# Reading the moving columns of float32r matmuls as two halves in turn, in a channel-attention and GELU-FFN kernel

## The chip, the core and the metric

The kernel runs on one NeuronCore of a Trainium2 chip. The metric is the device time of one execution, in microseconds (us). The engines are TensorE (PE in the profile; its weight loads are shown apart as PEld), VectorE (DVE), ScalarE (ACT), GpSimd (POOL, hardly used here) and SyncE (SP), whose queue issues the transfers between device memory and SBUF.

## The reference

For each of four batches an attention over channels, then a feed-forward net over all tokens:

```python
# q, k, v: (4, 6080, 256) float32; w_in: (256, 2048); w_out: (2048, 256)
qn = q / (norm(q, axis=1) + 1e-6)
kn = k / (norm(k, axis=1) + 1e-6)
s = kn.transpose(0, 2, 1) @ qn / tau          # (4, 256, 256): channels by channels
a = exp(s - s.max(-1)); a /= a.sum(-1) + 1e-9
x = (v @ a).reshape(24320, 256)
h = x @ w_in
out = (0.5 * h * (1 + erf(h / sqrt(2)))) @ w_out
```

## The kernel before

**The algebra.** The attention matrix `a` of a batch is multiplied into `w_in` first (`w_product`, L704 to L712), so that the two layers of the net are two products: v times the batch's own weights, then GELU, then `w_out`. Each value is held as a sum of two float32r numbers, a high and a low part, and a product of two such values is three matmuls: low weights by high columns, high by high, high by low. Those threes are the lines L885 to L887 (first layer), L1017 to L1019 (second layer), L1001 to L1003 (second layer, plain form), L829 to L831 and L963 to L965 (the first two chunks of the first batch), and L710 to L712. The scores of the batches after the first are summed by L460 and L462; those of the first batch use plain float32 matmuls (L417, L429).

**The tiling.** The 6080 tokens of a batch are cut into 12 chunks (`CHUNKS`), whose halves are 256 columns wide, and 240 in chunks 10 and 11. A chunk goes through four groups g = 0 to 3 of 512 hidden units. Chunks 0 and 1 of the first batch are done apart, in a simpler loop; the remaining 46 chunks make 184 groups (`steps`). In each group the first layer is computed by seven products instead of eight (a Strassen-Winograd scheme, `do`): 7 x 2 x 3 = 42 matmuls. The second layer has two forms:

- the *crossed* one (`CROSS`, L1017 to L1019), again seven products, 42 matmuls of 256 columns. It needs sums of the activations, which VectorE and ScalarE make (`t_add` L925 to L929, `t_hi` L932, `t_lo` L936), and four banks of PSUM that are joined at the chunk's end (`join_ops`);
- the *plain* one (L1001 to L1003), eight products as 24 matmuls of 512 columns, without those sums, needing one low part more (`lo`, L918).

`plain_out` says which form a group takes: all four groups of chunk (0, 2), and the last group of the chunks for which `MIXED` (L302) is true, which are those with b < 3 and odd c, and (3, 11).

**The order.** The second layer of a group is interleaved on TensorE with the first layer of the next (`row` and `outs` in the last loop). The products of the attention matrix, the score sums of the next batch and the preparation of the next chunk's v are put among the groups by `put(n, kind, ...)` and `spread(n, kind, time)`: a kind ("act0", "dve1", "o5", ...) names a place within the group. The plan gives the program order on which dependencies rest. TensorE keeps that order; for ScalarE, VectorE and the transfers, `Order.schedule` then simulates the plan with the costs of `Order.cost` (L108 to L134), lets each engine take the ready instruction that is due first, and writes the order found into the program. For a float32r matmul of k columns `cost` gives:

```python
return .4427 * k + 3.4 + 1.5 * (k <= H), .4427 * k + 170
```

**Names for the steps of the change.** `wins` holds a group's part of `w_in`, `whs`/`wls` the batch's weights, `vhi`/`vlo` a chunk's v with its sums, `his`/`los` the activations, `gs` the whole activations from which the low parts are taken, `hls` the split q and k. `sacc` is the score sum in SBUF, 256 columns for the high terms and 256 for the cross terms, which are added at L619. The moving operand of a matmul is its third argument; all of them run through their columns from the first to the last.

Of the kernel before, what the change touches and what calls it, by code (L numbers as in the profile page):

```python
# [13 lines left out]
ALU = mybir.AluOpType  # L14
# [3 lines left out]
B, N, C = 4, 6080, 256  # L18
DFF = 2048
# [59 lines left out]
class Order:  # L79
# [32 lines left out]
    def cost(self, ins, reads, writes):  # L112
        n = max([x[3] for x in reads + writes] + [1])
        psum = any(x[0][0] in ("pa", "pb", "px", "pz", "po0", "po1", "po2", "po3") for x in reads)
        if ins.engine == PE:
            k = reads[0][3] if reads else 1
            if ins.ins[0].dtype == F32:
                return (max(1.69 * k, 112.0),) * 2
            return .4427 * k + 3.4 + 1.5 * (k <= H), .4427 * k + 170
        if ins.engine == DVE:  # L120
            t = n / .96 + 66
            if type(ins).__name__ == "InstTensorCopy" and not psum:
                t = n / 1.92 + 66
            return t, t + 90
        if ins.engine == ACT:
            t = .855 * n + (48 if psum else 80)
            return t + 90 * (len(ins.outs) > 1), t + 105
        return 60, n * 512 / BANDWIDTH
# [171 lines left out]


def MIXED(b, c):  # L302
    return b < 3 and c % 2 or (b, c) == (3, 11)


NARROWS = (4, 9)
# [9 lines left out]
A21, B12 = -1, T1  # L316
PLAIN = (((1, 0), ((A11, B11), (A12, B21))), ((0, 0), ((A21, B11), (A22, B21))),
         ((1, 1), ((A11, B12), (A12, B22))), ((0, 1), ((A21, B12), (A22, B22))))


@with_exitstack
def channel_attention_gelu_ffn(ctx, tc, qk, kqt, vt, tau, w_in, w_out, out):
# [100 lines left out]
    def qk_fill():  # L423
        state["fill"] = s = ps_o.tile([P, NCT, C], F32, name="po0")
        for i in range(FILL * JS):
            js, j = divmod(i, JS)
            raw = raws[1, js]
            for m in range(NCT):
                marks["fill"] = nc.tensor.matmul(  # L429
                    s[:, m], raw[:, j, 0, m * P:(m + 1) * P], raw[:, j, 1], start=(i == 0 and m == 0),  # L430
                    stop=(i == FILL * JS - 1), skip_group_check=True)
                yield
        acc = state["sacc"] = pm.tile([P, NCT, NT], F32, name="sacc")
        nc.gpsimd.memset(acc[:, :, C:], 0.0)
        nc.vector.tensor_copy(out=acc[:, :, 0:C], in_=s)


    def sum_up(nps, acc, start, stop):
# [16 lines left out]
    def burst(b, k, m):  # L455
        cs = slice(m * P, (m + 1) * P)
        s = state["burst"] = spare()
        ops = [(hls[b, k * NB + t], j) for t in range(NB) for j in range(JS)]
        for i, (hl, j) in enumerate(ops):
            nc.tensor.matmul(s, hl[:, 0, j, 0, cs], hl[:, :, j, 1], start=(i == 0), stop=False,  # L460
                             skip_group_check=True)
            nc.tensor.matmul(s[:, 0:C], hl[:, 1, j, 0, cs], hl[:, 0, j, 1], start=False,  # L462
                             stop=(i == len(ops) - 1), skip_group_check=True)

    def burst_sum(k, m):
# [141 lines left out]
    def softmax(first, pool, name):  # L607
# [5 lines left out]
        for m in range(NCT):  # L613
            t = pm.tile([P, C], F32, name=f"t{m}")
            if first:
                nc.scalar.copy(out=t, in_=state["s"][m])
            else:
                s = state["sacc"]
                nc.vector.tensor_tensor(out=t, in0=s[:, m, 0:C], in1=s[:, m, C:2 * C], op=ALU.add)  # L619
            ts.append(t)  # L620
        nsum = state.pop("nsum")
        if first:
# [82 lines left out]
    def w_product(b, g, m, pwt):  # L705
        eh, el = state["e"]
        win = wins[b, g]
        cs = slice(m * P, (m + 1) * P)
        for d in range(NCT):
            nc.tensor.matmul(pwt, eh[:, d, cs], win[:, 0, d], start=(d == 0), stop=False)  # L710
            nc.tensor.matmul(pwt, eh[:, d, cs], win[:, 1, d], start=False, stop=False)
            nc.tensor.matmul(pwt, el[:, d, cs], win[:, 0, d], start=False, stop=(d == NCT - 1))  # L712

    def w_scale(tmp, m, pwt):
        nc.scalar.activation(out=tmp[:, 2 * m:2 * m + 2], in_=pwt.rearrange("p (q r c) -> p r q c", q=2, r=2),
# [109 lines left out]
    def product(u, a, v, ps, start, stop):  # L825
        g, q = divmod(u, 2)
        hi, lo = vops[v]
        wh, wl = (t[:, q] for t in w_slot(g, a))
        nc.tensor.matmul(ps, wl, hi, start=start, stop=False, skip_group_check=True)  # L829
        nc.tensor.matmul(ps, wh, hi, start=False, stop=False, skip_group_check=True)  # L830
        marks["product"] = nc.tensor.matmul(ps, wh, lo, start=False, stop=stop, skip_group_check=True)  # L831

    def gelu(src):
        at = state["at"] = (state.get("at", -1) + 1) % 5
# [26 lines left out]
    def chunk_ops(b, c, g, n):  # L861
# [11 lines left out]
        def do(i):  # L873
            a, v = ORDER[i]
            at = VSLOT[v]
            if i == 0:
                new("one", ps_h, "pb" if n % 2 else "pa")
            if i == 1:
                state["spare"] = "pa" if n % 2 else "pb"
                new("two", ps_h, state["spare"])  # L880
            ps = t[("one", "two", "one", "x", "one", "z", "one")[i]]
            for q in range(2):
                o = ps[:, q]
                start, stop = i < 2 and q == 0, i not in (0, 2, 4)
                nc.tensor.matmul(o, wls[g][:, a, q], vh[:, at, :h], start=start, stop=False, skip_group_check=True)  # L885
                nc.tensor.matmul(o, whs[g][:, a, q], vh[:, at, :h], start=False, stop=False, skip_group_check=True)  # L886
                nc.tensor.matmul(o, whs[g][:, a, q], vl[:, at, :h], start=False, stop=stop, skip_group_check=True)  # L887

        def x_copy():
            new("x", ps_x, "px")  # L890
# [59 lines left out]
    def pair_out(u, blocks):  # L950

        wo = wos[0, 0, u]
        t0, n = PAIRS[0]
        for j in range(2):
            for i in (1, 0):
                gh, gl = blocks[i, j]
                for c in range(NCT):
                    if u == 0 and i == 1:
                        po[j, c] = ps_o.tile([P, NT], F32, name=f"po{2 * j + c}")
                    o = po[j, c]  # L960
                    cs = slice(c * P, (c + 1) * P)
                    first, last = u == 0 and i == 1, u == NU - 1 and i == 0
                    nc.tensor.matmul(o, wo[:, 1, i, cs], gh, start=first, stop=False)  # L963
                    nc.tensor.matmul(o, wo[:, 0, i, cs], gh, start=False, stop=False)
                    nc.tensor.matmul(o, wo[:, 0, i, cs], gl, start=False, stop=last)  # L965
                    if last:
                        if c == 0:
                            osb = pg.tile([P, NCT, NT], F32, name="osb", bufs=1)
                            nc.scalar.copy(out=osb[:, 0], in_=o)
                        else:  # L970
                            nc.vector.tensor_copy(out=osb[:, 1], in_=o)
                            send(0, t0 + j * n, n, osb, osb)
                    yield

    def chunk_out(b, c, g, n):
# [13 lines left out]
        if plain_out(b, c, g):  # L989
            for i in (1, 0):  # L990
                for k in range(NCT):
                    form = {(0, 0): "A11", (0, 1): "A12", (1, 0): "A21", (1, 1): "A22"}[k, i]
                    for q in range(2):
                        def op(i=i, k=k, q=q, form=form):
                            w = wos[key + (form,)]
                            at = SLOT["B22"] if i else p_slot(n)
                            mh, ml = (m.rearrange("p i (q n) -> p i q n", q=2)[:, at:at + 2, q, :h] for m in (his, los))
                            start = first and i == 1 and q == 0
                            stop = last and i == 0 and q == 1
                            o = acc(k)  # L1000
# [7 lines left out]
        for i, (name, form, v) in enumerate(CROSS):  # L1008
            def op(i=i, name=name, form=form, v=v):
                k, half = PLACE[name]  # L1010
                o = acc(k)[:, half]
                w = wos[key + (form,)]
                starts = s_first and name in ("P3", "P4", "P1", "P5")
                stops = s_last and (k > 1 or last)
                for q in range(2):
                    mh, ml = (halves(m[:, SLOT[v]], h)[:, q] for m in (his, los))
                    nc.tensor.matmul(o, w[:, 1, q], mh, start=starts and q == 0, stop=False, skip_group_check=True)  # L1017
                    nc.tensor.matmul(o, w[:, 0, q], mh, start=False, stop=False, skip_group_check=True)  # L1018
                    nc.tensor.matmul(o, w[:, 0, q], ml, start=False, stop=stops and q == 1, skip_group_check=True)  # L1019
                if i % 2 or i == 6:  # L1020
                    load_part()
# [200 lines left out]
    for b in range(1, B):  # L1222
# [23 lines left out]
        for g in range(NWG):  # L1246
# [13 lines left out]
            for m in range(NCT):  # L1260
                put(n, "PE", product, m)
                put(n, "PEact", scale, m)
            put(n, "dve3", lambda tmp=tmp: w_adds(tmp["t"]))
            for i in range(2):
                put(n + 1, "act", lambda i=i, g=g, tmp=tmp: w_hi(g, tmp["t"], i))
                put(n + 1, "dve2", lambda i=i, g=g, tmp=tmp: w_lo(g, tmp["t"], i))
# [34 lines left out]
    for n, (b, c, g) in enumerate(steps):  # L1301
# [27 lines left out]
            put(n + 2, "dve1", ship, *((1,) if last else ()))  # L1329
        else:  # L1330
            put(n + 1, "o2", copy, 0)
            put(n + 1, "act2", copy, 2)
            put(n + 2, "act", copy, 3)
            put(n + 2, "dve1", join, "u1")
            put(n + 2, "dve1", join, "u23")
# [14 lines left out]
    for n, (b, c, g) in enumerate(steps):  # L1350
# [6 lines left out]
        for item in row:  # L1357
# [15 lines left out]
                e[item] = now + D  # L1373
            now += D
        assert not extra
        spread(n, "load", start + 0.02)
        spread(n, "act0", start + 0.03)
        spread(n, "dve0", start + 0.9)
# [10 lines left out]
        spread(n, "dve2", e[4] + .75)  # L1389
        spread(n, "o5", ends[5] + .05)  # L1390
        spread(n, "o2", ends[2] + .05)
        at(e[4] + .8, gelu_hi, "B11")
        at(e[4] + 1.3, gelu_whole, "B11")
        at(e[4] + 1.85, lo, "B11")
# [69 lines left out]
```

## Time and profile before

| | |
|---|---|
| median of 3 runs | 2144.01 us (2140.47 to 2144.54) |
| the profiled execution | 2140.3 us, its span 2138.5 us |
| granted TensorE clock, mean | 0.999 |
| matmul passes | 16444 |
| read from and written to device memory | 456.39 MB and 37.49 MB, 231 GB/s over the span |

The profile is of one execution. Its page gives each engine's busy time, and groups of instructions by line: tile written <- tiles read, number, busy time, mean duration of one, and the idle time of the engine just before them with what ended it. Matmuls overlap: one starts while the one before still drains, so the distance between two starts, not the printed duration, is what a pass takes of the engine. A float32 matmul shows as two passes; a float32r matmul as one. The timeline lists instructions by their start, the table of windows gives busy times in stretches of the span, and the list of waits says which instruction waited for which.

### The profile page before, as it was taken

How to read it: one execution, taken by the hardware profiler on the slowest of the kernel's cores; microseconds unless marked ns; L12 is line 12 of the kernel's file. 1: busy time of each engine (PE TensorE's matmuls, PEld its weight loads, DVE VectorE, ACT ScalarE, POOL GpSimd, SP SyncE). 2: the span in 40 equal slices, each digit the busy share in tenths (PEclk: the TensorE clock that was granted, in tenths of full speed). 3: DMA queues.
4: the chain of work that ended last, by engine and by line, in shares of the span. 5: the costliest groups of instructions: out<-in, count | busy, mean ns of one | idle time of the engine just before them, and what ended most of it. 6: DMA issues, size and time to landing. Idle time of an engine off the chain costs nothing.

```text
span 2138.5 us, 41862 instructions
## 1 busy us (share of the span) xinstructions
PE 2110.8 (99%) x16444; PEld 2035.4 (95%) x16444; DVE 1947.6 (91%) x2840; ACT 1656.4 (77%) x2768; POOL 1.3 (0%) x8
## 2 busy tenths in 40 slices
PE   8999999999999999999999999999999999999999
PEld 7788999999999999999999999999999999999999
DVE  6987999998899999999989999989999999999997
ACT  6656787788888888788887777777778777777776
POOL 0000000000000000000000000000000000000000
PEclk9999999999999999999999999999999999999999
DMA  9547777786887877877766666665566566656665
GB/s 380 184 125 265 266 252 247 273 273 211 273 283 244 279 245 248 276 235 269 255 216 227 217 230 209 224 215 198 197 208 218 186 197 211 230 193 223 220 202 185
DMA packets 159476, 496.61 MB, mean 232 GB/s; under 512 B 16304, under 2 KB 26544, under 8 KB 157232
## 3 DMA queue, kind: packets, MB, share of 16 engines
q1 hardware_dynamic: 159280, 493.94, 68.5%
q8 instruction: 129, 2.11, 0.4%
q14 instruction: 67, 0.55, 0.1%
HBM read 456.39 MB, written 37.49 MB: 231 GB/s over the span
## 4 chain that ended last, share of the span: by engine, by line
PE 88%; DVE 4%; DMA 4%; ACT 3%; issue 1%; SPq 0%; DVEq 0%; ACTq 0%
PE po L1017 12%; PE po L1019 12%; PE po L1018 12%; PE pa L885 5%; PE pb L885 5%; PE pa L887 5%; PE pa L886 5%; PE pb L887 5%; PE pb L886 5%; PE pz L887 2%; PE pz L885 2%; PE pz L886 2%; PE px L887 2%; PE px L885 2%; PE px L886 2%; PE pa L460 1%
## 5 line engine op out<-in xcount | busy, mean ns | idle before, releaser
L1017 PE MATMUL po<-his,wo 128*128 128x256 f32 (+1 forms) x2268 | 632.4, 279 | 1.5 <-DMA wo<-keep_out 1.4
L1019 PE MATMUL po<-los,wo 128*128 128x256 f32 (+1 forms) x2268 | 631.3, 278 | 0.3 <-DVE los L936 0.3
L1018 PE MATMUL po<-his,wo 128*128 128x256 f32 (+1 forms) x2268 | 631.3, 278 | 0.0
L932 ACT CAST his<-gs 128x1024 fp32r<-128x1024 f32 (+1 forms) x324 | 338.0, 1043 | 137.9 <-DVE gs L929 130.1
L918 DVE TENSOR_TENSOR los<-gs,his 128x512 fp32r<-128x512 f32 (+1 forms) x574 | 387.4, 683 | 54.8 <-ACT gs L912 40.2
L1017 PEld LDWEIGHTS po<-his,wo 128*128 128x128 f32 x2268 | 426.0, 188 | 5.6 <-DMA wo<-keep_out 2.1
L1018 PEld LDWEIGHTS po<-his,wo 128*128 128x128 f32 x2268 | 426.1, 188 | 0.8
L1019 PEld LDWEIGHTS po<-los,wo 128*128 128x128 f32 x2268 | 426.1, 188 | 0.6 <-DVE los L936 0.5
L936 DVE TENSOR_TENSOR los<-gs,his 128x1024 fp32r<-128x1024 f32 (+1 forms) x324 | 392.6, 1212 | 25.3 <-ACT his L932 23.3
L885 PE MATMUL pa<-vhi,wl 128*128 128x256 f32 (+1 forms) x920 | 257.3, 280 | 3.6 <-ACT gs L912 2.4
L885 PE MATMUL pb<-vhi,wl 128*128 128x256 f32 (+1 forms) x920 | 256.8, 279 | 3.3 <-ACT gs L912 1.6
L887 PE MATMUL pa<-vlo,wh 128*128 128x256 f32 (+1 forms) x920 | 256.0, 278 | 0.0
L887 PE MATMUL pb<-vlo,wh 128*128 128x256 f32 (+1 forms) x920 | 256.0, 278 | 0.0
L886 PE MATMUL pa<-vhi,wh 128*128 128x256 f32 (+1 forms) x920 | 255.9, 278 | 0.0
L886 PE MATMUL pb<-vhi,wh 128*128 128x256 f32 (+1 forms) x920 | 255.9, 278 | 0.0
L925 DVE TENSOR_TENSOR gs<-gs 128x1024 f32<-128x1024 f32 (+1 forms) x162 | 196.6, 1213 | 44.1 <-ACT gs L912 40.9
L885 PEld LDWEIGHTS pa<-vhi,wl 128*128 128x128 f32 x920 | 172.8, 188 | 8.9 <-ACT gs L912 3.0
L885 PEld LDWEIGHTS pb<-vhi,wl 128*128 128x128 f32 x920 | 172.8, 188 | 6.8 <-DVE pz L899 2.1
L886 PEld LDWEIGHTS pa<-vhi,wh 128*128 128x128 f32 x920 | 172.8, 188 | 2.5
L886 PEld LDWEIGHTS pb<-vhi,wh 128*128 128x128 f32 x920 | 172.8, 188 | 1.8
L887 PEld LDWEIGHTS pa<-vlo,wh 128*128 128x128 f32 x920 | 172.9, 188 | 0.0
L887 PEld LDWEIGHTS pb<-vlo,wh 128*128 128x128 f32 x920 | 172.9, 188 | 0.0
(286 smaller groups left out, 4718.2 us busy)
## 6 DMA issues: line engine op xcount, KB each, us to landing
wo<-keep_out SPq DMA_DIRECT2D x530, 512.0 KB, 4.5
raw<-qk SPq DMA_DIRECT2D x95, 512.0 KB, 6.3
wo<-keep_out SPq DMA_DIRECT2D x162, 256.0 KB, 4.0
kqc<-kqt SPq DMA_DIRECT2D x72, 512.0 KB, 5.2
v_raw<-vt SPq DMA_DIRECT2D x20, 1024.0 KB, 7.2
out<-osb SPq DMA_DIRECT2D x40, 512.0 KB, 5.6
win<-keep_in SPq DMA_DIRECT2D x12, 1024.0 KB, 7.2
keep_in<-win SPq DMA_DIRECT2D x4, 1024.0 KB, 4.6
```

The lines of the kernel that those rows point to most:

```text
L460: nc.tensor.matmul(s, hl[:, 0, j, 0, cs], hl[:, :, j, 1], start=(i == 0), stop=False, skip_group_check=True)
L885: nc.tensor.matmul(o, wls[g][:, a, q], vh[:, at, :h], start=start, stop=False, skip_group_check=True)
L886: nc.tensor.matmul(o, whs[g][:, a, q], vh[:, at, :h], start=False, stop=False, skip_group_check=True)
L887: nc.tensor.matmul(o, whs[g][:, a, q], vl[:, at, :h], start=False, stop=stop, skip_group_check=True)
L918: tt(out=slot(name)[1], in0=whole(name), in1=f32(slot(name)[0]), op=ALU.subtract)
L925: tt(out=g4[:, 0:2], in0=g4[:, 1:3], in1=g4[:, 0:2], op=ALU.subtract)
L932: nc.scalar.copy(out=views[1][:, 2 - 2 * i:4 - 2 * i], in_=views[0][:, 2 * i:2 * i + 2])
L936: tt(out=views[2][:, at], in0=views[0][:, 2 * i:2 * i + 2], in1=f32(views[1][:, at]), op=ALU.subtract)
L1017: nc.tensor.matmul(o, w[:, 1, q], mh, start=starts and q == 0, stop=False, skip_group_check=True)
L1018: nc.tensor.matmul(o, w[:, 0, q], mh, start=False, stop=False, skip_group_check=True)
L1019: nc.tensor.matmul(o, w[:, 0, q], ml, start=False, stop=stops and q == 1, skip_group_check=True)
```

## The change

Three things are done together.

First, a helper `paired` turns a run of n columns into the order 0, n/2, 1, n/2 + 1, ..., and the moving operand of each float32r matmul goes through it. The result of a matmul then stands in that order. To have it come out right, the host lays out the tokens of v in a matching order (twice undone, once per layer), and the columns of `w_in` within each 512; the score sum is put back where it is added up (L619), and the part of the second batch's scores that comes from plain float32 matmuls is brought into the same order when it is copied (L435). Stationary operands are read as before.

Second, `MIXED` is true everywhere, so the last group of every chunk takes the plain second layer.

Third, the planner's cost of a float32r matmul is changed, the four sums `w_adds` get a place "dve4" at the end of their group, and one copy of the crossed join gets a place "o3".

```diff
-            return .4427 * k + 3.4 + 1.5 * (k <= H), .4427 * k + 170
+            return .4167 * k + 3 + 1.5 * (k <= H), .4167 * k + 170
...
 def MIXED(b, c):
-    return b < 3 and c % 2 or (b, c) == (3, 11)
+    return True
...
+def paired(ap):
+    return ap.rearrange("p (a b) -> p b a", a=2)
...
-        nc.vector.tensor_copy(out=acc[:, :, 0:C], in_=s)
+        for m in range(NCT):
+            nc.vector.tensor_copy(out=acc[:, m, 0:C].rearrange("p (b a) -> p b a", a=2), in_=paired(s[:, m]))
...
-            nc.tensor.matmul(s, hl[:, 0, j, 0, cs], hl[:, :, j, 1], start=(i == 0), stop=False,
+            nc.tensor.matmul(s, hl[:, 0, j, 0, cs], hl[:, :, j, 1].rearrange("p h (a b) -> p h b a", a=2), start=(i == 0), stop=False,
                              skip_group_check=True)
-            nc.tensor.matmul(s[:, 0:C], hl[:, 1, j, 0, cs], hl[:, 0, j, 1], start=False,
+            nc.tensor.matmul(s[:, 0:C], hl[:, 1, j, 0, cs], paired(hl[:, 0, j, 1]), start=False,
...
-                nc.vector.tensor_tensor(out=t, in0=s[:, m, 0:C], in1=s[:, m, C:2 * C], op=ALU.add)
+                both = s[:, m].rearrange("p (h b a) -> p h a b", h=2, a=2)
+                nc.vector.tensor_tensor(out=t.rearrange("p (a b) -> p a b", a=2), in0=both[:, 0], in1=both[:, 1],
+                                        op=ALU.add)
...
-                nc.tensor.matmul(o, wls[g][:, a, q], vh[:, at, :h], start=start, stop=False, skip_group_check=True)
-                nc.tensor.matmul(o, whs[g][:, a, q], vh[:, at, :h], start=False, stop=False, skip_group_check=True)
-                nc.tensor.matmul(o, whs[g][:, a, q], vl[:, at, :h], start=False, stop=stop, skip_group_check=True)
+                nc.tensor.matmul(o, wls[g][:, a, q], paired(vh[:, at, :h]), start=start, stop=False, skip_group_check=True)
+                nc.tensor.matmul(o, whs[g][:, a, q], paired(vh[:, at, :h]), start=False, stop=False, skip_group_check=True)
+                nc.tensor.matmul(o, whs[g][:, a, q], paired(vl[:, at, :h]), start=False, stop=stop, skip_group_check=True)
...
-                            mh, ml = (m.rearrange("p i (q n) -> p i q n", q=2)[:, at:at + 2, q, :h] for m in (his, los))
+                            mh, ml = (m.rearrange("p i (q n) -> p i q n", q=2)[:, at:at + 2, q, :h].rearrange(
+                                "p i (a b) -> p i b a", a=2) for m in (his, los))
...
-                    mh, ml = (halves(m[:, SLOT[v]], h)[:, q] for m in (his, los))
+                    mh, ml = (paired(halves(m[:, SLOT[v]], h)[:, q]) for m in (his, los))
...
-            put(n, "dve3", lambda tmp=tmp: w_adds(tmp["t"]))
+            put(n, "dve4", lambda tmp=tmp: w_adds(tmp["t"]))
...
-            put(n + 1, "act2", copy, 2)
+            put(n + 1, "o3", copy, 2)
...
+        spread(n, "dve4", now - 0.02)
...
+        spread(n, "o3", ends[3] + .05)
...
-        "vt": np.ascontiguousarray(np.asarray(v).reshape(B * N, C).T),
+        "vt": np.ascontiguousarray(np.asarray(v).reshape(B * N, C).T[:, tokens]),
...
-        "w_in": np.ascontiguousarray(moe_w_in).view(np.int64),
+        "w_in": np.ascontiguousarray(np.asarray(moe_w_in)[:, columns]).view(np.int64),
```

The lines L710 to L712, L829 to L831 and L963 to L965 get `paired` around their moving operand in the same way.

More of the change, by code (lines that the diff above doesn't have):

```diff
@@ L709, in w_product @@
         for d in range(NCT):
-            nc.tensor.matmul(pwt, eh[:, d, cs], win[:, 0, d], start=(d == 0), stop=False)
-            nc.tensor.matmul(pwt, eh[:, d, cs], win[:, 1, d], start=False, stop=False)
-            nc.tensor.matmul(pwt, el[:, d, cs], win[:, 0, d], start=False, stop=(d == NCT - 1))
+            nc.tensor.matmul(pwt, eh[:, d, cs], paired(win[:, 0, d]), start=(d == 0), stop=False)
+            nc.tensor.matmul(pwt, eh[:, d, cs], paired(win[:, 1, d]), start=False, stop=False)
+            nc.tensor.matmul(pwt, el[:, d, cs], paired(win[:, 0, d]), start=False, stop=(d == NCT - 1))
     def w_scale(tmp, m, pwt):
@@ L828, in product @@
         wh, wl = (t[:, q] for t in w_slot(g, a))
-        nc.tensor.matmul(ps, wl, hi, start=start, stop=False, skip_group_check=True)
-        nc.tensor.matmul(ps, wh, hi, start=False, stop=False, skip_group_check=True)
-        marks["product"] = nc.tensor.matmul(ps, wh, lo, start=False, stop=stop, skip_group_check=True)
+        nc.tensor.matmul(ps, wl, paired(hi), start=start, stop=False, skip_group_check=True)
+        nc.tensor.matmul(ps, wh, paired(hi), start=False, stop=False, skip_group_check=True)
+        marks["product"] = nc.tensor.matmul(ps, wh, paired(lo), start=False, stop=stop, skip_group_check=True)
     def gelu(src):
@@ L962, in pair_out @@
                     first, last = u == 0 and i == 1, u == NU - 1 and i == 0
-                    nc.tensor.matmul(o, wo[:, 1, i, cs], gh, start=first, stop=False)
-                    nc.tensor.matmul(o, wo[:, 0, i, cs], gh, start=False, stop=False)
-                    nc.tensor.matmul(o, wo[:, 0, i, cs], gl, start=False, stop=last)
+                    nc.tensor.matmul(o, wo[:, 1, i, cs], paired(gh), start=first, stop=False)
+                    nc.tensor.matmul(o, wo[:, 0, i, cs], paired(gh), start=False, stop=False)
+                    nc.tensor.matmul(o, wo[:, 0, i, cs], paired(gl), start=False, stop=last)
                     if last:
@@ L1446, with pairs @@
     kqt = qk.reshape(B, P, NJ, 2 * C).transpose(0, 3, 2, 1)
+    def pairs(n, times=1):
+        x = np.arange(n)
+        for _ in range(times):
+            x = x.reshape(n // 2, 2).T.reshape(n)
+        return x
+    tokens = [t + i * n + pairs(n, 2) for b in range(B) for c, (t0, h) in enumerate(CHUNKS)
+              for t, n, m in [(b * N + t0, *((2 * h, 1) if b == 0 and c < 2 else (h, 2)))] for i in range(m)]
+    tokens = np.concatenate(tokens)
+    columns = (np.arange(0, DFF, NT)[:, None] + pairs(NT)).reshape(DFF)
     arrays = {
```

## The prediction

> **What bounds the kernel now.** I read the page first (span, busy time, chain of waits), then the table of windows, then the list of waits, then the timeline of the matmuls themselves.
>
> ```profile
> span 2138.5 us, 41862 instructions
> ...
> PE 2110.8 (99%) x16444; PEld 2035.4 (95%) x16444; DVE 1947.6 (91%) x2840; ACT 1656.4 (77%) x2768; POOL 1.3 (0%) x8
> ...
> PE 88%; DVE 4%; DMA 4%; ACT 3%; issue 1%; SPq 0%; DVEq 0%; ACTq 0%
> ```
> ```profile
> 0.00:60.00 60.00, 53.74 (x245) 45.34 (x246) 42.83 (x69) 36.71 (x52) 1.31 (x8) 1.00 0.98 382
> ...
> 78.00:160.00 82.00, 82.00 (x359) 67.09 (x358) 73.18 (x137) 52.01 (x93) 0.00 (x0) 1.00 0.43 135
> ...
> 600.00:1000.00 400.00, 398.18 (x3162) 387.70 (x3161) 370.78 (x520) 331.97 (x550) 0.00 (x0) 1.00 0.76 256
> ...
> 1800.00:2100.00 300.00, 300.00 (x2569) 300.00 (x2568) 282.43 (x395) 230.50 (x386) 0.00 (x0) 1.00 0.64 212
> ```
> ```profile
> PE pa L417 <- DMA raw<-qk: 5.4, 4, 3.4
> PE pb L460 <- ACT p L895: 4.2, 4, 1.7
> ```
>
> The columns of a window are PE, PEld, DVE and ACT busy, POOL, the granted clock, the DMA share and GB/s. TensorE is the bound: 99% busy, 88% of the chain, without a pause from 1800 to 2100 us, and its two longest waits are 5.4 and 4.2 us in all. VectorE is next, at 371 of 400 us. So the time is the number of matmul passes times the distance between their starts. That distance is not the printed duration (about 280 ns, which overlaps the next pass), so it is read from start times:
>
> ```profile
> 1002.07 0.28 PE L885 MATMUL pb<-vhi,wl 128*128 128x256 f32 x1
> ...
> 1004.07 0.28 PE L887 MATMUL pa<-vlo,wh 128*128 128x256 f32 x1
> ...
> 1009.47 0.40 PE L460 MATMUL pb<-hl 128*128 128x512 f32 x1
> ...
> 1010.51 0.39 PE L460 MATMUL pb<-hl 128*128 128x512 f32 x1
> ```
> ```profile
> 343.54 0.28 PE L885 MATMUL pa<-vhi,wl 128*128 128x256 f32 x1
> ...
> 344.22 0.39 PE L1001 MATMUL po<-his,wo 128*128 128x512 f32 x1
> ```
> ```profile
> 2079.85 0.28 PE L1017 MATMUL po<-his,wo 128*128 128x240 f32 x1
> ...
> 2080.52 0.27 PE L885 MATMUL pa<-vhi,wl 128*128 128x240 f32 x1
> ```
> ```profile
> 40.18 0.59 PE L417 MATMUL pa<-raw 128*128 128x256 f32 x2
> ...
> 44.50 0.59 PE L417 MATMUL pa<-raw 128*128 128x256 f32 x2
> ```
> ```profile
> 49.49 0.19 PEld L440 LDWEIGHTS po<-ones,acc 128*128 128x128 f32 x1
> ```
> ```profile
> 50.94 0.19 PEld L440 LDWEIGHTS po<-ones,acc 128*128 128x128 f32 x1
> ```
>
> From 1002.07 to 1004.07 lie 17 distances between float32r passes of 256 columns: 2.00 / 17 = **117.6 ns**. From 1009.47 to 1010.51 lie three passes of 512 and three of 256: 1.04 / 3 = 347, less 117.6, gives **229 to 230 ns** for 512. In the stretch at 343 us six passes of 256 take 0.68 us, **113.3 ns** each, with the same instruction and the same columns. Passes of 240 columns: 0.67 / 6 = **111.7 ns**. A plain float32 matmul (L417) makes two passes over its 256 columns; 20 passes take 4.32 us, **216 ns** each. And the sums of L440 stream one column against fresh 128-column weights: 13 weight loads in 1.45 us, **111.5 ns** each. That is the least that a pass with weights of its own has cost here.
>
> These rows carry the argument. The float32 pass reads its columns at half speed, and half of 216 is 108 ns, so a float32r pass of 256 loses about 10 ns somewhere that the slow reader doesn't. The stretch at 343 us loses only 5, so the loss isn't in the arithmetic: it hangs on how the reads fall. The granted clock is 1.00 in these windows, so it isn't the clock either.
>
> **The change, part by part.** (1) Every float32r pass reads column 0, then column n/2, then 1, then n/2+1. Each half is then read at half the pace, which is what the float32 pass does with its one run, and there the loss is absent. If the memory can serve two runs in turn, the loss goes. No row shows such a pass. Bounds: as fast as 108 ns by half the float32 pass, but the weight load holds it at 111.5, so 110 to 111.7 is the near end; the far end is 216 ns, one column at the pace of the float32 pass. I take **111.6 ns**, the weight-load row, since the 240-column pass already sits there. For the same reason the 240-column passes gain nothing. For 512 columns the ends are 216 (two of 108) and 230; I take **217**, and for 480 in proportion 203.5 against 215.5 (both x 480/512).
>
> ```profile
> L1018 PE MATMUL po<-his,wo 128*128 128x256 f32 x1876 | 523.9, 279 | 0.0
> ...
> L886 PE MATMUL pb<-vhi,wh 128*128 128x256 f32 x760 | 212.1, 279 | 0.0
> ...
> L886 PE MATMUL px<-vhi,wh 128*128 128x256 f32 x304 | 84.9, 279 | 0.0
> ...
> L1002 PE MATMUL po<-his,wo 128*128 128x512 f32 x144 | 56.7, 394 | 0.0
> L460 PE MATMUL pb<-hl 128*128 128x512 f32 x136 | 50.1, 402 | 4.2 <-ACT p L895 4.2
> ...
> L462 PE MATMUL pb<-hl 128*128 128x256 f32 x136 | 38.1, 280 | 0.0
> ...
> L964 PE MATMUL po<-his,wo 128*128 128x512 f32 x64 | 25.1, 392 | 0.0
> ```
>
> Passes of 256: L885 to L887 have 760 into each of pa and pb and 304 into each of px and pz, so 2128 x 3 = 6384; L1017 to L1019 have 1876 x 3 = 5628; L462 has 136 x 2 = 272. Together 12,284. Passes of 512: L460 272, L1001 to L1003 432, L829 to L831 and L963 to L965 192 each, L710 to L712 192: 1280. Passes of 480: 32 x 3 = 96. The saving is 12,284 x 6.1 ns = 74.9 us, 1280 x 13 = 16.6 us, 96 x 12 = 1.2 us: **92.7 us**, all on the engine that sets the end. Some 5 us of it lie in 78 to 160 us, where VectorE is busy 73 of 82 us and may keep a part.
>
> [...]
>
> (2) The last group of each chunk takes the plain second layer. It does so now in 18 chunks (b below 3, c odd, and (3, 11)) besides chunk (0, 2); after it in all, so 27 groups are new, 4 of them 240 columns wide. A crossed group costs 42 narrow passes in its second layer, a plain one 24 of double width: 24 x 217 - 42 x 111.6 = +0.52 us, times 23, and 24 x 203.5 - 42 x 111.7 = +0.2 us, times 4: **+12.8 us** on TensorE, 486 instructions fewer.
>
> ```profile
> L936 DVE TENSOR_TENSOR los<-gs,his 128x1024 fp32r<-128x1024 f32 x268 | 327.9, 1224 | 19.1 <-ACT his L932 17.6
> L918 DVE TENSOR_TENSOR los<-gs,his 128x512 fp32r<-128x512 f32 x474 | 322.3, 688 | 42.0 <-ACT gs L912 30.3 <-ACT his L915 2.6
> L925 DVE TENSOR_TENSOR gs<-gs 128x1024 f32<-128x1024 f32 x134 | 164.1, 1225 | 35.0 <-ACT gs L912 32.4
> L927 DVE TENSOR_TENSOR gs<-gs 128x512 f32<-128x512 f32 x134 | 92.0, 687 | 1.0
> L929 DVE TENSOR_TENSOR gs<-gs 128x512 f32<-128x512 f32 x134 | 91.8, 685 | 0.3
> ...
> L619 DVE TENSOR_TENSOR t<-sacc 128x256 f32<-128x256 f32 x6 | 2.5, 420 | 0.0
> ```
>
> VectorE loses in each such group one L925, one L927, one L929 and two L936 and gains one L918: 1.225 + 0.687 + 0.685 + 2 x 1.224 - 0.688 = 4.36 us, some 117 us in all; the chunk's join costs it about 0.3 us more each time. ScalarE loses two casts of L932 and a copy for one more L915. Each group loads 1.0 MB of weights where it loaded 1.75. None of this is on the path now, so it counts nothing by itself. It is the cover: in 600 to 1000 us VectorE works 371 us. TensorE's 400 become about 384; half of the nine chunks there are newly plain, so VectorE falls to some 352 and keeps the same share. Without part (2) it would need 371 of 381, and every wait of VectorE for ScalarE would show on TensorE.
>
> (3) The copies in and out of the score sum (L435, now two, and L619) read or write in steps of two. There are 6 of 420 ns and one pair; between no cost and double that is 0 to 3 us, beside matmuls in all batches but the first. I take nothing. (4) Moved steps: the four sums L741 to L744 are put later in their group, at the planner's new place "dve4"; they issue no DMA. The "o3" copy stands in a branch that no last group reaches any more. The new numbers in the planner's cost only order instructions; I take no duration from them. Reordering could move TensorE's pauses, 1.8 us in 600 to 1000 and none in 1800 to 2100, by a few us either way: 0, with 15 us up and 10 us down kept for the range.
>
> **Sum**: -92.7 + 12.8 = -79.9 us. The profiled execution took 2140.3 us (its span 2138.5), so 2060.4; the median shown, 2144.0, is 3.7 us above that execution, and carried over gives 2064. I say **2062 us**.
>
> **Rivals.** *A: the loss stays.* If the 10 ns come from something other than the run being read (from the weights read beside it, say), narrow passes stay at 117.6 and only the plain layer counts: 23 x (24 x 230 - 42 x 117.6) + 4 x (24 x 215.5 - 42 x 111.7) = 13.4 + 1.9: **2156 us, slower**. It decides as soon as a narrow pass gains under 15.3 us / 12,284 = 1.2 ns. For it: 113.3 and 117.6 ns occur with the same columns, so something beside them matters. Against it: the float32 pass loads the same weights and has no loss. *B: every column opens anew.* If the reader holds one place at a time, alternating costs it on each column. At the float32 pass's pace, 216 ns: 12,284 x 98 + 2520 x 91 + 1280 x 202 + 96 x 190 ns = 1.71 ms, and 27 x 24 x 432 - 27 x 42 x 216 ns = 0.04 ms: about **3890 us**. No row of before reads two places in turn on TensorE, so nothing excludes it; that passes of L460, over two separate runs, keep 230 ns speaks only for one jump. *C: half the gain.* The pass stops at the 113.3 ns of the stretch at 343 us, and 512 columns at 229: 54 + 1.3 - 19 us gives **2104 us**.
>
> [...]
>
> **How the numbers follow.** Forecast 0.74, C 0.11, A 0.09, B 0.06. The forecast's own range is 2030 to 2090: downwards 110 ns for 256 columns and 216 for 512 (another 21 us) with fewer pauses, upwards 15 us of new pauses, the 5 us that VectorE may keep, and the median's 4. Up to 2110 it takes in C; 0.95 of 0.74 and nearly all of 0.11 make 0.8. A measurement of this kernel tells about 0.2% (4 us) from no change. Faster: the forecast and C, 0.85. A lies 0.5% above; a little of it, 0.02, falls within 0.2%. Slower 0.13.
>
> **What would show it.** The distance of narrow passes in the changed trace: 111 to 112 ns says forecast, 113.3 C, 117.6 A, near 216 B. Passes of 240 columns should stay at 111.7; if they fall below 110, the weight load doesn't hold them and the time comes out lower. Passes of 512 should stand at 216 to 219. VectorE should show some 1835 us, and TensorE waits for VectorE or ScalarE no longer than now; a PE row with tens of us of idle before it, released by L918 or L912, would say that the cover was too thin. I am wrong if the two halves meet in the same part of the memory, which the trace of before can't show.

## The result, and the profile after

The changed kernel takes 2087.67 us (median of 4 runs, 2082.17 to 2090.00) against 2142.74 us: a ratio of **0.974, 95% interval 0.9718 to 0.9762**. A later job gave 2087.83 us and 0.975 (0.9734 to 0.9766). The profiled execution took 2087.4 us, 52.9 less than that of before; the sum had 79.9 less.

The page after, its span, its busy times and its chain of waits:

```profile
span 2085.4 us, 40663 instructions
...
PE 2039.9 (98%) x15958; PEld 1967.0 (94%) x15958; DVE 1857.6 (89%) x2733; ACT 1621.0 (78%) x2718; POOL 1.3 (0%) x8
...
PE 83%; DVE 7%; ACT 4%; DMA 4%; issue 2%; SPq 0%; DVEq 0%; ACTq 0%
```

Lines of the changed kernel stand 5 (weight splitting), 7 (groups) or 8 (second layer) further down than before: L530 is now L535, L918 is L925, L936 is L943, L1017 is L1025. TensorE has 486 passes fewer, as counted. But its share of the chain fell from 88 to 83%, and VectorE's rose from 4 to 7%: part of the end is now set elsewhere. The timeline of the matmuls after, for passes of 256, 512 and 240 columns:

```profile
1002.13 0.28 PE L1025 MATMUL po<-his,wo 128*128 128x256 f32 x1
...
1003.92 0.28 PE L1026 MATMUL po<-his,wo 128*128 128x256 f32 x1
```
```profile
567.04 0.38 PE L718 MATMUL pa<-win,eh 128*128 128x512 f32 x1
...
567.69 0.38 PE L718 MATMUL pa<-win,eh 128*128 128x512 f32 x1
```
```profile
2030.02 0.28 PE L1025 MATMUL po<-his,wo 128*128 128x240 f32 x1
...
2031.92 0.28 PE L1027 MATMUL po<-los,wo 128*128 128x240 f32 x1
```

From 1002.13 to 1003.92 lie 16 distances: 1.79 / 16 = 112 ns, where there were 117.6. Three passes of 512 columns take 0.65 us, 217 ns each (216 is the median over all). Seventeen distances at 240 columns take 1.90 us, 112 ns: unchanged, and the same as at 256. So each pass got what was forecast. What was lost lies between the passes. The table of windows after (columns as before: PE, PEld, DVE, ACT, POOL, clock, DMA, GB/s):

```profile
78.00:160.00 82.00, 75.06 (x333) 63.80 (x333) 78.78 (x136) 52.38 (x90) 0.00 (x0) 0.96 0.41 129
...
200.00:600.00 400.00, 390.57 (x3131) 378.71 (x3131) 357.69 (x528) 331.15 (x565) 0.00 (x0) 1.00 0.76 256
600.00:1000.00 400.00, 397.91 (x3223) 387.27 (x3223) 371.13 (x525) 331.20 (x551) 0.00 (x0) 1.00 0.74 252
```

In 78 to 160 us TensorE, which had been busy throughout (82.00), now pauses 7 us, while VectorE rose from 73.18 to 78.78 of 82.

To count the pauses I take, for each pass, the distance to the next start less the median distance of passes of its kind and width, and add up what is over 8 ns (so passes at a slower pace count too). Before: 35.7 us, 12.2 of them up to the first pass of the first group (at 160.2 us) and 23.5 after it. In the changed kernel: **65.1 us, 22.8 and 42.3** (first group at 165.4 us). The pauses grew by 29.4 us; the spans differ by 53.1; so what is left to the passes themselves is 82.5 us, where the sum had 79.9.

### The profile page after: what moved, and what is told of

Its sections match the earlier page's. It is cut to its first block, busy times and chain, and to the rows that moved or that the text cites. A ratio compares the mean times of both kernels' runs of the same rounds, so it can differ in the third digit from the quotient of the medians.

```text
span 2085.4 us, 40663 instructions
## 1 busy us (share of the span) xinstructions
PE 2039.9 (98%) x15958; PEld 1967.0 (94%) x15958; DVE 1857.6 (89%) x2733; ACT 1621.0 (78%) x2718; POOL 1.3 (0%) x8
## 4 chain that ended last, share of the span: by engine, by line
PE 83%; DVE 7%; ACT 4%; DMA 4%; issue 2%; SPq 0%; DVEq 0%; ACTq 0%
PE po L1027 9%; PE po L1026 9%; PE po L1025 9%; PE pb L892 4%; PE pb L894 4%; PE pb L893 4%; PE pa L892 4%; PE pa L894 4%; PE pa L893 4%; PE po L1009 3%; PE po L1011 3%; PE po L1010 3%; PE pz L894 2%; PE pz L893 2%; PE pz L892 2%; DMA v_raw<-vt 2%
## 5 line engine op out<-in xcount | busy, mean ns | idle before, releaser
L1027 PE MATMUL po<-los,wo 128*128 128x256 f32 (+1 forms) x1890 | 520.9, 276 | 1.0 <-DVE los L943 0.8
L1025 PE MATMUL po<-his,wo 128*128 128x256 f32 (+1 forms) x1890 | 520.5, 275 | 0.8 <-issue 0.8
L1026 PE MATMUL po<-his,wo 128*128 128x256 f32 (+1 forms) x1890 | 520.0, 275 | 0.0
L925 DVE TENSOR_TENSOR los<-gs,his 128x512 fp32r<-128x512 f32 (+1 forms) x601 | 406.7, 683 | 83.0 <-ACT gs L919 71.0
L1025 PEld LDWEIGHTS po<-his,wo 128*128 128x128 f32 x1890 | 362.9, 192 | 2.8 <-ACT e L669 0.9
L1027 PEld LDWEIGHTS po<-los,wo 128*128 128x128 f32 x1890 | 363.1, 192 | 2.0 <-DVE los L943 1.5
L1026 PEld LDWEIGHTS po<-his,wo 128*128 128x128 f32 x1890 | 363.1, 192 | 0.5
L943 DVE TENSOR_TENSOR los<-gs,his 128x1024 fp32r<-128x1024 f32 (+1 forms) x270 | 326.7, 1211 | 16.3 <-ACT his L939 14.0
L939 ACT CAST his<-gs 128x1024 fp32r<-128x1024 f32 (+1 forms) x270 | 281.3, 1043 | 64.6 <-DVE gs L936 59.5
L892 PE MATMUL pa<-vhi,wl 128*128 128x256 f32 (+1 forms) x920 | 254.2, 276 | 8.1 <-ACT gs L919 7.3
L892 PE MATMUL pb<-vhi,wl 128*128 128x256 f32 (+1 forms) x920 | 254.6, 277 | 4.8 <-DVE pz L906 1.4
L932 DVE TENSOR_TENSOR gs<-gs 128x1024 f32<-128x1024 f32 (+1 forms) x135 | 163.8, 1214 | 31.6 <-ACT gs L919 27.5
L892 PEld LDWEIGHTS pa<-vhi,wl 128*128 128x128 f32 x920 | 176.5, 192 | 13.4 <-ACT gs L919 8.3
L922 ACT ACTIVATE his<-px 128x512 fp32r<-128x512 f32 (+1 forms) x184 | 109.0, 592 | 101.7 <-PE px L894 98.6
L892 PEld LDWEIGHTS pb<-vhi,wl 128*128 128x128 f32 x920 | 176.7, 192 | 10.0 <-DVE pz L906 2.6
```

The source lines that it names most:

```text
L892: nc.tensor.matmul(o, wls[g][:, a, q], paired(vh[:, at, :h]), start=start, stop=False, skip_group_check=True)
L922: nc.scalar.activation(out=slot(name)[0], in_=t[SOURCE[name]], func=AF.Gelu)
L925: tt(out=slot(name)[1], in0=whole(name), in1=f32(slot(name)[0]), op=ALU.subtract)
L932: tt(out=g4[:, 0:2], in0=g4[:, 1:3], in1=g4[:, 0:2], op=ALU.subtract)
L939: nc.scalar.copy(out=views[1][:, 2 - 2 * i:4 - 2 * i], in_=views[0][:, 2 * i:2 * i + 2])
L943: tt(out=views[2][:, at], in0=views[0][:, 2 * i:2 * i + 2], in1=f32(views[1][:, at]), op=ALU.subtract)
```

## The experiments

Two theories stood at the start. One: the paired reads give what was forecast, and VectorE, which has too little room at the faster pace, takes part of it back. The other: the planner's new order, or the time before the first group, gives it back, and the plain second layer only costs. Pauses are given as "up to the first group / after it".

| kernel | median, us | ratio to before, 95% interval | pauses, us |
|---|---|---|---|
| changed kernel | 2087.67 | 0.974 (0.9718 to 0.9762) | 22.8 / 42.3 |
| pair_only | 2131.73 | 0.9951 (0.9936 to 0.9966) | 26.3 / 94.4 |
| plain_only | 2149.68 | 1.0034 (1.0022 to 1.0047) | 13.3 / 16.6 |
| old_costs | 2092.27 | 0.9772 (0.9758 to 0.9787) | 25.8 / 43.4 |
| early_plain | 2083.40 | 0.973 (0.9715 to 0.9744) | 16.6 / 43.3 |
| early_blocks | 2088.91 | 0.976 (0.9743 to 0.9777) | 24.2 / 41.7 |
| evens | 4065.59 | 1.8992 (1.8952 to 1.9033) | 9.8 / 1.8 |
| ways4 | 2534.82 | 1.1841 (1.1816 to 1.1867) | 10.3 / 10.7 |
| pair_no_vlo | 2083.91 | 0.9735 (0.9713 to 0.9757) | 26.0 / 45.8 |
| changed_again | 2087.83 | 0.975 (0.9734 to 0.9766) | 25.1 / 42.3 |
| floor_costs | 2078.81 | 0.9712 (0.9696 to 0.9728) | 23.5 / 33.0 |
| early_dve | 2088.62 | 0.9753 (0.9737 to 0.9769) | 24.0 / 42.7 |
| plain_floor | 2074.22 | 0.9688 (0.9671 to 0.9705) | 16.5 / 32.2 |

### Each half of the change alone

pair_only, on the changed kernel:

```diff
 def MIXED(b, c):
-    return True
+    return b < 3 and c % 2 or (b, c) == (3, 11)
```

> The changed kernel with the plain second layer only where it was before (b < 3 and odd c, and (3, 11)): the paired reads alone. The passes should stand at 111.6 ns (256 and 240 columns) and 216 ns (512), so TensorE has 13 us less to do than in the changed kernel. Theory (the plain layer is the cover: VectorE has too little room without it): pauses of TensorE grow by more than that, total 2085 to 2115 us, long waits for los and gs in the chunks that are crossed throughout. Rival (the pauses of the changed kernel lie in the first 165 us and in the order alone, and the plain layer only costs): about 2075 us.

plain_only, on the kernel before:

```diff
 def MIXED(b, c):
-    return b < 3 and c % 2 or (b, c) == (3, 11)
+    return True
```

> The kernel before with the plain second layer in the last group of every chunk, and nothing else. Passes keep 117.6 and 230 ns. Theory: 27 groups cost 0.55 us more each and VectorE's room is not needed at this pace: 2156 us, 0.6 per cent slower than before. Rival (TensorE's pauses of before, 20 us after the first 165 us, go when VectorE has less to do): 2140 to 2146 us.

The paired reads alone gain half a per cent, the plain layer alone costs a third of one, and both together gain 2.6. The passes of pair_only have the changed kernel's medians (112 and 216 ns), so nothing is lost there; its pauses after the first group are 94.4 us against 23.5 before. Both its theories had too low a time, the first by 17 us. The table of windows of pair_only, then the same window of the kernel before, in the last batch, where almost every group is crossed:

```profile
1650.00:2050.00 400.00, 383.38 (x3354) 378.33 (x3353) 377.05 (x524) 309.36 (x509) 0.00 (x0) 1.00 0.64 210
```
```profile
1650.00:2050.00 400.00, 399.34 (x3358) 397.84 (x3357) 377.24 (x527) 309.18 (x514) 0.00 (x0) 1.00 0.63 207
```

TensorE does 3354 passes in 400 us with the faster reads and 3358 without: not one more. VectorE works 377 us in both. That is 377.24 / 3358 = 112.3 ns of VectorE for each pass (112.4 in pair_only), and a pass now takes TensorE 112: in this stretch VectorE has as much to do as TensorE, and its 94% (377.24 of 400 us) left no room for faster passes. The list of TensorE's waits in pair_only names what is late, the low parts of the sums:

```profile
PE po L1027 <- DVE los L943: 12.7, 27, 1.0
```

plain_only came out at +8.0 us where 15 had been worked out. Its pauses fell by 5.8 us, so the plain layer's price is about what was worked out, and part of it is returned in pauses; the time lies between the two theories.

### Load or chain

VectorE can be late because it has too much to do, or because the chain through ScalarE and VectorE inside a group is too long. pair_no_vlo, on pair_only, takes away VectorE work that lies outside that chain.

```diff
     def v_lo(b, c, part):
         src, hi, lo = v_part(b, c, part)
+        if b:
+            return
         nc.vector.tensor_tensor(out=lo, in0=src, in1=f32(hi), op=ALU.subtract)
```

> The kernel with the paired reads alone (plain second layer only where it was before), without the low parts of v in the batches after the first, which leaves out 2.1 us of VectorE work per chunk that no group waits for within its own chain. Theory (after the paired reads VectorE's sheer load is the bound in crossed chunks): the pauses go for the most part, some 34 x 1.5 us less, about 2080 us. Rival (the chain through ScalarE and VectorE within each group is too long for the faster passes, whatever VectorE's load): no change, 2125 to 2133 us.

It took 48 us off pair_only, and the pauses after the first group fell from 94.4 to 45.8. In 1650 to 2050 us its TensorE does 3561 passes:

```profile
1650.00:2050.00 400.00, 398.86 (x3561) 397.93 (x3561) 372.41 (x506) 322.12 (x538) 0.00 (x0) 1.00 0.69 219
```

VectorE now has 372.41 / 3561 = 104.6 ns to do for each pass. So less load is enough, without a shorter chain. That a shorter chain would help too wasn't tried: in pair_only 15 of the 23 us in which VectorE idles in this window are waits for ScalarE's steps within the groups. Less load is also what the plain layer buys in the changed kernel: 4.36 us of VectorE per group for half a microsecond of TensorE.

### The stage before the first group

In this stage VectorE splits the raw 64-bit weights, with operations that read or write every second word (`raw`). Grouped by line and form in 78 to 165 us, the changed kernel has

```profile
L529 DVE SCALAR_TENSOR_TENSOR raw<-raw,kqc 128x512 uint32<-128x512 uint32 x6 | 5.6, 926 | 0.0
L535 DVE SCALAR_TENSOR_TENSOR kqc<-raw 128x512 f32<-128x512 uint32 x6 | 5.4, 894 | 0.0
```

and the kernel before, for the second of them,

```profile
L530 DVE SCALAR_TENSOR_TENSOR kqc<-raw 128x512 f32<-128x512 uint32 x6 | 4.1, 686 | 0.0
```

The same operation takes 894 ns in place of 686. Two kernels ask whether the reads do it. early_plain reads the first two chunks, which run in this stage, in plain order:

```diff
-        nc.tensor.matmul(ps, wl, paired(hi), start=start, stop=False, skip_group_check=True)
-        nc.tensor.matmul(ps, wh, paired(hi), start=False, stop=False, skip_group_check=True)
-        marks["product"] = nc.tensor.matmul(ps, wh, paired(lo), start=False, stop=stop, skip_group_check=True)
+        nc.tensor.matmul(ps, wl, hi, start=start, stop=False, skip_group_check=True)
+        nc.tensor.matmul(ps, wh, hi, start=False, stop=False, skip_group_check=True)
+        marks["product"] = nc.tensor.matmul(ps, wh, lo, start=False, stop=stop, skip_group_check=True)
...
-    tokens = [t + i * n + pairs(n, 2) for b in range(B) for c, (t0, h) in enumerate(CHUNKS)
+    tokens = [t + i * n + pairs(n, 0 if m == 1 else 2) for b in range(B) for c, (t0, h) in enumerate(CHUNKS)
```

(and the same in L970 to L972).

> The changed kernel, but the two layers of the first two chunks (those with passes of 512 columns, before the first group) read their columns in the plain order again. Theory (VectorE's operations on every second word of the raw weights, 880 to 930 ns in the changed kernel against 686 before, are slowed by TensorE's paired reads of halves 1024 bytes apart): these operations are back at 686 ns, the first group starts at about 160 us instead of 165.4, total some 5 us less, 2082 us. Rival (VectorE is merely late because TensorE is faster, and its longer durations come from elsewhere): they stay near 900 ns and the first group stays at 163 to 166 us.

early_blocks keeps two halves in turn there, but within each block of 256 columns, with the layout to match:

```diff
+def blockwise(ap):
+    return ap.rearrange("p (h a b) -> p h b a", h=2, a=2)
```

> The changed kernel, but in the first two chunks a pass of 512 columns reads its two blocks of 256 one after the other, each as two halves in turn, so the halves lie 512 bytes apart instead of 1024. Theory (two runs read in turn slow VectorE's operations on every second word, whatever the distance): these stay near 900 ns, the first group starts at about 165 us, total as the changed kernel, 2083 to 2091 us. Rival (the distance of 1024 bytes matters): they are back at 686 ns with passes at 216 ns, the first group starts at about 159 us, total about 2081 us.

In early_plain the operation is back:

```profile
L535 DVE SCALAR_TENSOR_TENSOR kqc<-raw 128x512 f32<-128x512 uint32 x6 | 4.1, 676 | 0.0
```
```profile
78.00:160.00 82.00, 81.50 (x358) 66.85 (x357) 74.97 (x139) 54.45 (x97) 0.00 (x0) 1.00 0.43 135
```

TensorE is busy 81.5 of 82 us again, with slower passes, and the first group starts at 161.6 us instead of 165.4. In early_blocks the operation (there L539) takes 851 ns and the first group starts at 166.9 us, so halving the distance of the halves doesn't bring 686 ns back. Both theories in front held: beside these reads the operation takes 894 and 851 ns, beside reads in plain order 676. Order and pace change together here (512 columns in 216 ns in place of 230), and no run takes the two apart: ways4, which also reads in turn but needs 281 ns, leaves this operation at 684 ns. Nor is the effect confined to VectorE's operations on every second word: in this stage ScalarE's L524, which reads such words, takes 912 ns in place of 674, and VectorE's L847, on contiguous data, 754 in place of 688 (744 in pair_only, 698 in early_blocks). All in all the 160 VectorE operations that split the weights and serve the first two chunks take 113.3 us, where they took 97.3. In the groups VectorE's operations on contiguous data did not become longer: L925 takes 689 ns on 512 elements, where it took 688 (as L918).

One pause there is paid twice. The timeline of the changed kernel, with the idle time before an instruction at the end of its row:

```profile
133.89 0.80 PE L970 MATMUL po<-his,wo 128*128 128x512 f32 x1 [4.44 <-DVE wo L539]
134.48 0.63 PE L971 MATMUL po<-his,wo 128*128 128x512 f32 x1
134.91 0.63 PE L972 MATMUL po<-los,wo 128*128 128x512 f32 x1
135.33 0.63 PE L970 MATMUL po<-his,wo 128*128 128x512 f32 x1
...
137.47 0.63 PE L972 MATMUL po<-los,wo 128*128 128x512 f32 x1
```

TensorE waits 4.4 us for the split weights, and the passes after it stand 427 ns apart ((137.47 - 134.91) / 6) instead of 216. The row of the window from 78 to 160 us shows the granted clock at 0.96, and at 1.00 in early_plain; from 134 to 138 us of the changed kernel it was 0.50.

### The plan

old_costs gives the planner the cost of before; floor_costs gives it what the passes take:

```diff
-            return .4167 * k + 3 + 1.5 * (k <= H), .4167 * k + 170
+            return max(.4167 * k + 2.7, 111.6), .4167 * k + 170
```

> The changed kernel with the planner's old cost of a float32r pass (118 and 230 ns), so only the order of ScalarE, VectorE and the transfers differs. Theory (the pauses in the groups come from chains of VectorE and ScalarE with little room, not from a wrong cost in the plan): within 5 us of the changed kernel, 2083 to 2093 us. Rival (the order made with the new cost is what gives the 25 us back): 2070 us or less.

> The changed kernel with the planner told the passes as they were measured: 111.6 ns for 256 and for 240 columns, 216 for 512 (the changed kernel's plan takes 104.5 ns for 240). Theory (the remaining pauses come from VectorE's load and from the joints between batches, not from the plan): within 4 us of the changed kernel. Rival (the plan hurries TensorE too much in the chunks of 240 columns and orders badly): 2075 us or less, with fewer waits near 500 to 530 and 1020 to 1050 us.

early_dve puts the four sums of the weights back from "dve4" to "dve3".

> The changed kernel with the four sums of the batch's weights put back to their old place in the plan (dve3 in place of dve4). Theory (the list scheduler orders VectorE by due times, so the place hardly matters): within 3 us of the changed kernel. Rival (the place at the group's end keeps VectorE free for the groups' own chain): 5 to 10 us slower.

changed_again is the changed kernel in the same job as floor_costs, early_dve and plain_floor.

> The changed kernel itself, beside the three others of this job on one chip. 2083 to 2090 us by every theory; it is the measure for the others.

The place of the sums makes no difference (2088.6 against 2087.8). The old cost takes 4.6 us more than the changed kernel's, in different jobs and with intervals that overlap; that is within its theory. But the measured cost takes 9.0 us less, in one job and with intervals that do not overlap (0.9696 to 0.9728 and 0.9734 to 0.9766); the pauses after the first group fall from 42.3 to 33.0 us. The theory had no room for that; the rival was right in kind and too hopeful in size. The new cost of the changed kernel is 104.5 ns for 240 columns, which take 111.6, and 111.2 for 256. That the 240 columns alone do it wasn't tried.

About half of the 9 us is the pace of passes after a pause. The timeline of the changed kernel, then the window around it, then the same window of floor_costs:

```profile
1029.53 0.28 PE L1027 MATMUL po<-los,wo 128*128 128x240 f32 x1
1033.02 0.57 PE L892 MATMUL pa<-vhi,wl 128*128 128x240 f32 x1 [3.21 <-ACT gs L919]
1033.38 0.42 PE L893 MATMUL pa<-vhi,wh 128*128 128x240 f32 x1
...
1035.72 0.42 PE L892 MATMUL pb<-vhi,wl 128*128 128x240 f32 x1
```
```profile
1000.00:1100.00 100.00, 96.61 (x778) 94.43 (x777) 84.54 (x132) 86.71 (x150) 0.00 (x0) 0.98 0.73 248
```
```profile
1000.00:1100.00 100.00, 96.12 (x775) 92.95 (x775) 86.22 (x143) 81.32 (x142) 0.00 (x0) 1.00 0.68 222
```

After 3.2 us without a pass, passes of 240 columns stand (1035.72 - 1033.38) / 11 = 213 ns apart in place of 112; from 1033 to 1036 us the granted clock was 0.50. The changed kernel has two more such stretches after its first group, at 224 us (behind a wait of 3.8 us) and at 1156 us (behind 1.1 us), with the clock at 0.50 from 224 to 227 and from 1156 to 1159 us. In changed_again the three add 5.1 us to the pauses; floor_costs, whose longest wait there is 2.3 us, has none (its mean granted clock is 0.998, that of changed_again 0.993). What decides which pauses are followed by slow passes these runs don't settle.

### Why two halves

> The changed kernel with another order of columns in every float32r pass: first the even columns, then the odd ones, layouts following. Neighbours in the order are never neighbours in memory, but each stretch of memory is passed at twice the pace and twice. Theory (the loss of before comes with the pace at which one stretch of memory is passed, and halving it is what cures): the loss doubles, 512 columns take about 246 ns and 256 about 125 ns, total about 2280 us. Rival (any order without neighbours cures it): 216 and 111.6 ns, 2083 to 2092 us.

evens, on the changed kernel, with the layouts following:

```diff
 def paired(ap):
-    return ap.rearrange("p (a b) -> p b a", a=2)
+    return ap.rearrange("p (b a) -> p a b", a=2)
```

> The changed kernel with four quarters in turn instead of two halves, layouts following. Theory (two runs already take the loss away, and the weight load holds the narrow passes): passes stay at 111.6 and 216 ns, total 2083 to 2092 us. Rival (each further run costs the reader a new place): 512 columns above 220 ns, total above 2100 us.

ways4:

```diff
 def paired(ap):
-    return ap.rearrange("p (a b) -> p b a", a=2)
+    return ap.rearrange("p (a b) -> p b a", a=4)
```

Passes of 512 columns on the timeline of evens, and of ways4:

```profile
99.53 0.63 PE L836 MATMUL pa<-vhi,wl 128*128 128x512 f32 x1
...
102.25 0.63 PE L836 MATMUL px<-vhi,los 128*128 128x512 f32 x1
```
```profile
99.94 0.44 PE L836 MATMUL pa<-vhi,wl 128*128 128x512 f32 x1
...
102.47 0.45 PE L970 MATMUL po<-his,wo 128*128 128x512 f32 x1
```

2.72 / 6 = 453 ns with even columns first, 2.53 / 9 = 281 ns with four quarters in turn; 216 with two halves, 230 with one run. For evens neither theory held: steps of two along one run cost about twice the time per column (453 ns against 230), near rival B's price, where the theory had 246 ns. For ways4 the rival held: four runs cost a third more than two (281 ns against 216). Of the four orders that ran, two runs in turn is the best, and four are not better still; why, no run shows.

### A faster version

plain_floor joins the two edits that helped, early_plain and floor_costs.

> The kernel with the first two chunks read in plain order and the planner told the measured passes. Theory: the gain of the plain order there stands, some 4 us less than the changed kernel, 2079 to 2085 us, and the planner's cost adds nothing. Rival (both gains add): 2075 us or less.

It takes **2074.22 us, 0.9688 (0.9671 to 0.9705) of before**, 13.6 us less than the changed kernel in the same job. The gains add: in this job floor_costs took 9.0 us off, and the plain order takes 4.6 more; early_plain alone, in another job, was 4.3 us below the changed kernel, with intervals that overlap. Its pauses are 16.5 and 32.2 us.

## Why the prediction was right, and where it was off

**The number.** The forecast was 2062 us; 2087.67 is 25.7 us more. That is inside the stated 2090, but beyond the 2086 to which its allowances add up (15 us of pauses, 5 for VectorE, 4 for the median). So the direction and the pass times were foreseen, and that the time stayed in the forecast's own range is partly luck.

**The pass.** Narrow passes were forecast at 111.6 ns, held there by the weight load, 240 columns without gain, 512 columns at 217. Measured: 112, 112 and 217 by the rows above (216 is the median). That the weight load holds them was my reading of the 111.5 ns of L440 in the kernel before, and the changed kernel fits it: behind a pass of 480 or 512 columns, passes of 256 (those of the score sums, L467, and of L892) have a median of 109 ns and passes of 240 (L892) one of 102, against 112 behind narrow passes. So 111.5 ns is not the least that a pass with weights of its own takes. That the float32 pass reads at half speed was an estimate from its 216 ns for 256 columns beside 117.6; the 108 ns drawn from it lie near that 109. The reason given, that each run is read at half the pace, isn't borne out: four quarters are each read more slowly still, and take 281 ns. That two halves gain was right; why they do stays open.

**The count.** -92.7 + 12.8 = -79.9 us for the passes; 82.5 by the account of spans and pauses. plain_only bears out the second term with its passes unchanged.

**The term that failed** is part (4), "TensorE's pauses ... 0, with 15 us up and 10 us down kept for the range". It was +29.4 us. 10.6 of them fell before the first group, where I let VectorE keep up to 5 us of the gain and didn't foresee that its own operations would become slower (L530's 686 ns became 894). (The 160 operations counted above make up 16 of the 22.6 us by which VectorE's 1857.6 exceeds the forecast 1835.) The other 18.8 came in the groups; some 9 of them go with a plan that knows the passes' true cost, and 4.5 are passes at half pace (213 ns for 240 columns in place of 112) behind three waits, which go with that plan too; the rest is not taken apart. Part (3), counted as nothing, cost VectorE 0.6 us: L625 and L440 take 3.8 us, where L619 and L435 took 3.2.

**The cover.** I wrote that part (2) counts nothing by itself and is the cover, and that VectorE without it "would need 371 of 381". The role was right, but it was given no price: without the plain layer the pauses grow by another 55.6 us (26.3 + 94.4 less 65.1). The step that failed is taking VectorE's load from 600 to 1000 us, where half of the chunks had the plain layer already, and calling 371 of 381 a load that still fits. In the last batch VectorE has 112.3 ns to do for each pass, which leaves nothing beside a pass of 111.6; what looks idle there is mostly waiting for ScalarE (15 of 23 us in pair_only). The sign that was named for a thin cover, one row of TensorE with tens of us of idle before it, did not show: the longest single wait of the changed kernel is 4.4 us, and pair_only's largest row, L1027 behind L943, has 12.7.

**The rivals.** A (the loss stays) is refuted by the passes: 112 ns, where A had 117.6. B is refuted for two halves; its price came up in another order, even columns first: evens has a median of 227 ns for passes of 256 columns, where B had 216, and 453 for 512, where B had 432. C gave 2104 us by a slower pass; the time came out between it and the forecast for another reason.

## What to carry to other kernels

Where one engine is the bound and another is busy over 90%, take the gain of the first only as far as the second can follow: divide the second's busy time by the first's passes, in the stretch where it has most to do, and compare that with the new time of a pass (here 112.3 ns and 112). Test each half of a paired change alone: here one half was worth 10 us, the other cost 8, and both gave 55. Read the pace of matmuls from their start times by width, and the floor from a pass that streams almost nothing: here its 111.5 ns told ahead that passes of 240 columns, at 111.7, would stay (112). When a pass becomes faster, give the planner its measured cost, floors included: here that took 9.0 us off.

## What the runs showed of the hardware that was not expected

- The time of a float32r pass of 512 columns went with the order in which it read them: 230 ns in one run, 216 as two halves in turn, 281 as four quarters, 453 as even columns and then odd ones.
- In the stage where TensorE read 512 columns as two halves in turn, VectorE's L529 and L535, on every second word, took 926 and 894 ns in place of 685 and 686, and ScalarE's L524 912 in place of 674; within blocks of 256 columns (halves 512 bytes apart in place of 1024) the first two took 841 and 851. An operation on contiguous data beside them (L847) took 754 ns in place of 688, and 698 with the blocks; in the groups such operations stayed as they were (688 and 689 ns). With four quarters, where a pass takes 281 ns, L535 took 684 ns, L524 686 and L847 688.
- After 4.4 us without a matmul, passes of 512 columns stood 427 ns apart in place of 216 for some 4 us; after 3.2 us, passes of 240 columns 213 ns apart in place of 112 for some 3 us. The granted clock was 0.50 in both stretches.
